# Expert 0's first three columns listed from the early rows, the rest of its list finished under its first layer, and gathers spread behind units and products

## The chip, the cores and the metric

One core of a Trainium2 chip runs the whole kernel. Its engines are TensorE (PE), VectorE (DVE), ScalarE (ACT), GpSimd (POOL) and SyncE (SP); each takes its instructions in its own order, and semaphores tie the orders together. The metric is the device time of one execution in microseconds (us), the median of three runs.

## The reference

```python
def _attn_ref(q, k, v, tau):                      # B, N, C = 4, 5056, 256
    qn = q / (norm(q, axis=1) + 1e-06);  kn = k / (norm(k, axis=1) + 1e-06)
    s = kn.transpose(0, 2, 1) @ qn / tau          # 256 x 256 for each batch
    a = exp(s - s.max(-1));  a /= a.sum(-1) + 1e-09
    return v @ a                                  # x: 4 * 5056 = 20224 rows of 256

def _moe_ref(x, w_gate, w1, w2):                  # E = 8 experts, F = 1024
    cap = N // E                                  # 2528 tokens for each expert
    order = argsort(-(x @ w_gate).flatten())
    # in this order a (token, expert) pair is taken if the token is free
    # and the expert has fewer than cap tokens
    for e in range(E):
        out[assigned == e] = maximum(x[assigned == e] @ w1[e], 0) @ w2[e]
```

Every token so goes to exactly one expert, and each expert gets exactly 2528 tokens.

## The kernel before, in words

**Attention.** The four batches' scores are made first, then the rows x = v @ a in 20 chunks of 1024 rows (`CH`), eight row tiles each (`px` products, L295; ACT copies them to `xs`, L298). ACT issues a store of every four tiles to `x_d` in DRAM (L308). The last eight chunks run in the order of `TODO`, and while they run, the routing of expert 0 is made beside them.

**Routing.** For expert p the cut of the capacity is searched on DVE, with counts summed over the partitions by small PE products (`pc`, L860 and L873). Then `compact(p)` turns the mask of 128 x 160 tokens into a list: 20 columns of 128 row numbers (`src`) and output positions (`idx`). For each column a PE product (`pi`) and a test on 160 elements with an accumulator give the position; ACT does 9 columns of the first list (L1091) and DVE 11 (L1107); some 20 small DVE operations then make `src` (L1175 to L1203) and `idx`. The list of expert p+1 is made under the products of expert p.

**Experts.** A chunk is up to four columns of 128 tokens. POOL gathers a column's rows from `x_d` with an indirect DMA (L1498, after a tiny `spacer` memset, L1497); `turn` transposes them (L1646 on PE for some chunks, DVE for others) and splits them in a high and a low part, `xH` and `xL` (L1656, L1659). `layer1` has eight units, each of six products into a `ph` buffer (L1693); ACT writes the relu's high part `hH` (L1696) and DVE the rest `hL` (L1702). `layer2` has 24 products for each column (L1742), an ACT copy to `y` (L1751), and an indirect DMA of POOL that scatters the rows to the output (L1754). For experts 4 to 7 some chunks take a variant with fewer products (`layers`, `PARTED`, `MIXED`). Expert p+1's two weight matrices come by indirect DMA on POOL too (L1390, 1 MB each), and ACT and DVE split them in a high and a low part (L1399, L1403).

**What sets the order.** A planner, `Order`, keeps an estimated clock for PE and DVE (`o.pe`, `o.dve`). Side streams (routing, lists) yield the engine and cost of their next piece, and are woven between the products where the planner thinks that the piece's inputs are ready by `o.margin` ns. `o.until(key)` runs a stream to its end at this place. Gathers wait in a list, `queue`; each call of `gather(after)` issues the next one, behind the given instruction. Before, they were called behind units of `layer1`, after scatters of `layer2`, and, in `turn` for experts with 1 in `MIXED`, all that were queued at once.

**The seam** is the place where attention ends and expert 0 begins. Before, `o.until(("idx", 0))` ended the whole first list there; then the first two columns were gathered, 26 `warm` products on an identity (L1672) ran on PE, and `turn(0, 0)` transposed the two columns with four more warm products between them. All gathers read the whole of `x_d`, so the first one waits for the last store.

Of the kernel before, what the change touches and what calls it, by code (L numbers as in the profile page):

```python
# [21 lines left out]
E, F = 8, 1024  # L22
# [11 lines left out]
FEW = 3  # L34
BY_V = 9
NACT = 9
# [7 lines left out]
PAIRS = (((0, 4), (1, 0)), ((1, 1), (1, 2)), ((1, 3), (1, 4)), ((2, 0), (2, 1)), ((2, 2), (2, 3)),  # L44
         ((2, 4), (3, 0)), ((3, 1), (3, 2)), ((3, 3), (3, 4)))
# [21 lines left out]
TODO = ((1, 1), (1, 3), (1, 4), (3, 1), (3, 2), (3, 3), (3, 4), (3, 0), (2, 0), (2, 1), (2, 2), (2, 3), (2, 4))  # L67
CUT = (4, 4, 4, 4, 4)
FIRST_CUT = (2, 4, 4, 4, 4, 2)
# [6 lines left out]
FIRST_MARGIN = 150  # L76
# [10 lines left out]
START_TICKS = 26  # L87
FILL = (4, 1)
# [22 lines left out]
def attention_moe(ctx: ExitStack, tc: tile.TileContext, q, k, vt, tau, wg, w1t, w2t, tabs, out):  # L111
# [193 lines left out]
    def store_x(b, c, xs, t0, t1):  # L305
        r0 = (b * NCH + c) * CH
        rows = x_d[r0:r0 + CH].rearrange("(p t) c -> p t c", t=T)
        nc.scalar.dma_start(rows[:, t0:t1], xs[:, t0 % TH:t0 % TH + t1 - t0, 0:C])  # L308

    with ExitStack() as sctx:  # L310
# [265 lines left out]
        late(logits, 4, behind_ac)  # L576
# [3 lines left out]
        for n in (6, 7, 5):  # L580
            late(logits, n)
# [33 lines left out]
    def route(p, R):  # L615
# [10 lines left out]
        else:  # L626
# [34 lines left out]
            for q in range(Q):  # L661
                yield (vi if q else ve)(COLS, 4)
                V.tensor_scalar(oh[:, q], f, float(E - q), None, op0=OP.is_equal)
            if few:
                need = rtile("need", (128, E))
                yield ve(R)
                V.tensor_scalar(need[:, 0:R], ne[:, 0, 0:R], row0, None, op0=OP.mult)
                yield ve(R)
                V.tensor_copy(need[:, 4:3 + R], need[:, 0:R - 1])
                yield ve(1)  # L670
                V.tensor_scalar(need[:, 3 + R:4 + R], need[:, R - 1:R], 2.0, float(COLS), op0=OP.mult, op1=OP.add)
                cnt = rtile("cnt", (128, 16))
                yield ve(R)
                V.memset(cnt[:, 3 * R:4 * R] if R > 2 else cnt, 0.0)
            else:
# [18 lines left out]
            def masked(keys, r0, r1):  # L694
                n = r1 - r0
                M = oh[:, 3:3 + n].bitcast(I16)
                if "only" not in r:
                    r["only"] = True
                    yield ve(n * COLS, 4)
                    V.tensor_scalar(M, oh[:, r0:r1], 2.0 * HALF - 1.0, -HALF, op0=OP.mult, op1=OP.add)  # L700
                mine = oh[:, 5:5 + n].bitcast(I16)
                yield ve(n * COLS, 2)
                V.tensor_tensor(mine, keys[:, None, :].to_broadcast([128, n, COLS]), M, op=OP.min)
                r["keys"] = mine
# [12 lines left out]
            def summed(slots, at):  # L717
                Ec = rtile("Ec", (128, 16), F32R)
                n = slots * R
                yield ve(n)  # L720
                V.tensor_tensor(Ec[:, 0:n].rearrange("p (j r) -> p j r", r=R), cnt[:, 0:n].rearrange("p (j r) -> p j r", r=R),
                                need[:, None, at:at + R].to_broadcast([128, slots, R]), op=OP.add)
# [3 lines left out]
                r["tot"] = pc[:, 0:n].rearrange("p (j r) -> p j r", r=R)  # L726

            def counts(tests, slots):
# [6 lines left out]
                yield from summed(slots, 0)  # L735

            def search_few(keys):
                cur = None
                own = rtile("Gf")
                yield vi(64 + COLS)  # L740
                V.scalar_tensor_tensor(own, keys, HALF, oh[:, R - 1], op0=OP.add, op1=OP.mult)
                yield from masked(keys, 0, R - 1)
                for i in range(8):
                    if i == 0:
                        thr = rtile("thr", (128, NT, CG), I16, bufs=2)[:, 0:3]
                        yield vi(3 * CG)
                        V.tensor_copy(thr, steps2[:, 0, 0:3, None].to_broadcast([128, 3, CG]))
                    bias = rtile("bias", (128, 8), bufs=2)[:, 0:3]
                    yield ve(3)
                    V.tensor_scalar(bias, thr[:, :, 0], -1.0, 0.5 - HALF, op0=OP.mult, op1=OP.add)  # L750
                    by_act = aside(own, bias, [cnt[:, j * R + R - 1:j * R + R] for j in range(3)])
                    yield from tested_by(thr, 3, cnt[:, 0:3 * R].rearrange("p (j r) -> p j r", r=R)[:, :, 0:R - 1])
                    while not by_act:
                        yield "W", 0
                    yield from summed(4, 4)
                    mx = rtile("mxc", (128, 3))
                    yield ve(3 * R, psum=True)
                    V.tensor_reduce(mx, r["tot"][:, 0:3, :], axis=AX.X, op=OP.max)
                    hit = rtile("hitc", (128, 3))
                    n = rtile("n_hit", (128, 1))  # L760
                    yield ve(64 + 3)
                    V.tensor_scalar(hit, mx, 0.0, 0.0, op0=OP.is_ge, op1=OP.add, accum_out=n)
                    step = float(1 << 14 - 2 * i)
                    new = rtile("cur", (128, 1), bufs=2)
                    yield ve(1)
                    if i == 0:
# [4 lines left out]
                    if i < 7:  # L771
                        thr = rtile("thr", (128, NT, CG), I16, bufs=2)[:, 0:3]
                        yield ve(3 * CG)
                        V.tensor_scalar(thr, steps2[:, i + 1, 0:3, None].to_broadcast([128, 3, CG]), cur, None, op0=OP.add)
# [32 lines left out]
            def search_one(keys):  # L807
# [5 lines left out]
                yield from masked(keys, 2, 3)  # L813
# [195 lines left out]
        r["G"] = ramps[p]  # L1009
        yield ve(COLS, 0.5)  # L1010
# [581 lines left out]
    def turn(p, c):  # L1592
        while any(e[:2] == (p, c) for e in queue):
            gather()
# [38 lines left out]
        if not by_v:  # L1633
# [5 lines left out]
            if not head:  # L1639
                steps.sort()  # L1640
# [417 lines left out]
```

## Time and profile before

| | |
|---|---|
| median of 3 runs | 1255.12 us (1254.25 to 1255.97) |
| the profiled execution's own time | 1257.65 us |
| its span (first to last instruction of the trace) | 1255.9 us |
| mean granted TensorE clock | 0.996 |
| PE busy | 1231.2 us, 98% |
| DVE busy | 933.7 us, 74% |
| ACT busy | 646.9 us, 52% |
| POOL busy | 382.9 us, 30% |

The profiled execution is 2.5 us above the median, and 1.75 us of its own time lie outside its span. Busy time of PE holds idle time within it, because matmuls are pipelined and their ends are modelled: a chain of 256-column products shows durations of some 0.28 us but starts one every 0.115 us. Where PE waits, the row of a timeline has the idle time before it in brackets, with what ended it.

### The profile page before, as it was taken

What the parts mean: (1) busy time and instruction counts of PE and PEld (TensorE: products, weight loads), DVE (VectorE), ACT (ScalarE), POOL (GpSimd) and SP (SyncE); (2) the same over time, 40 slices, a digit from 0 to 9 for tenths busy, and PEclk for the clock granted to TensorE, in tenths of its full rate; (3) what the DMA queues carried; (4) which work ended last, traced back from release to release, by engine and by line L of the source; (5) the groups of instructions that cost most, each with busy time, mean ns of one, the idle gap of its engine ahead of it and who ended that gap; (6) DMA issues with size and microseconds to landing.
All of it is one profiled execution on the core that took longest, in us unless ns stands there. A gap on an engine that the chain in (4) does not pass through costs nothing.

```text
span 1255.9 us, 23692 instructions
## 1 busy us (share of the span) xinstructions
PE 1231.2 (98%) x8710; PEld 1100.2 (88%) x8710; DVE 933.7 (74%) x2396; ACT 646.9 (52%) x1491; POOL 382.9 (30%) x693
## 2 busy tenths in 40 slices
PE   9999999999999999999999999999999999998998
PEld 7879977898888988988899899989989888988898
DVE  6688597798778777867867888887787777674752
ACT  5646653467324443524533755547663646563652
POOL 0000000001532363254443434433434443343422
PEclk9999999999999999999999999999999999998999
DMA  8999875436233144353533543463554362554420
GB/s 309 305 408 415 320 261 195 156 156 252 60 76 109 53 111 134 81 127 100 155 97 81 138 105 88 114 143 100 118 134 111 109 159 76 117 114 109 100 52 33
DMA packets 223812, 184.62 MB, mean 147 GB/s; under 512 B 152656, under 2 KB 193488, under 8 KB 219088
## 3 DMA queue, kind: packets, MB, share of 16 engines
q1 hardware_dynamic: 196624, 103.66, 29.7%
q0 software_dynamic: 17664, 58.22, 14.6%
q10 hardware_dynamic: 9408, 21.24, 4.4%
q8 instruction: 68, 1.11, 0.4%
q14 instruction: 48, 0.39, 0.1%
HBM read 123.30 MB, written 59.77 MB: 146 GB/s over the span
## 4 chain that ended last, share of the span: by engine, by line
PE 74%; issue 11%; POOL 6%; DMA 5%; DVE 2%; ACT 2%; POOLq 0%; SPq 0%; ACTq 0%; DVEq 0%
PE py L1742 26%; PE ph L1693 24%; PE px L295 8%; PE s L347 8%; POOL out_dram L1754 3%; DMA x_d<-xs 2%; POOL xg L1498 2%; PE pc L860 2%; PE ph L1783 2%; DMA ua<-in_q_dram 1%; PE py L1783 1%; PE px L473 1%; DMA uc<-in_k_dram 1%; PE pi L1073 1%; DMA uc<-in_q_dram 1%
## 5 line engine op out<-in xcount | busy, mean ns | idle before, releaser
L1742 PE MATMUL py<-uc,hH 128*128 128x256 f32 (+1 forms) x2560 | 341.1, 281 | 5.5 <-ACT y L1751 3.0
L1742 PEld LDWEIGHTS py<-uc,hH 128*128 128x128 f32 (+1 forms) x2560 | 316.5, 188 | 8.3 <-ACT y L1751 3.2
L1693 PE MATMUL ph<-xH,ua 128*128 128x512 f32 (+3 forms) x928 | 250.3, 387 | 0.5 <-DVE hL L1702 0.4
L1696 ACT ACTIVATE hH<-ph 128x512 fp32r<-128x512 f32 (+3 forms) x232 | 134.0, 580 | 145.9 <-PE ph L1693 134.7
L1754 POOL DMA_INDIRECT out_dram<-y,idx x105 | 109.0, 1038 | 296.9 <-ACT y L1751 270.9
L1498 POOL DMA_INDIRECT xg<-x_d,src x156 | 153.7, 985 | 138.1 <-ACT hH L1696 57.7
L1693 PEld LDWEIGHTS ph<-xH,ua 128*128 128x128 f32 x928 | 166.8, 188 | 30.4 <-DVE hL L1702 0.6
L1702 DVE SCALAR_TENSOR_TENSOR hL<-ph,hH 128x512 fp32r<-128x512 f32 (+3 forms) x232 | 153.7, 664 | 43.1 <-ACT hH L1696 36.1
L1742 PE MATMUL py<-uc,hL 128*128 128x256 f32 (+1 forms) x1280 | 181.8, 281 | 0.0
L1742 PEld LDWEIGHTS py<-uc,hL 128*128 128x128 f32 (+1 forms) x1280 | 162.4, 188 | 0.1
L1693 PE MATMUL ph<-xL,ua 128*128 128x512 f32 (+3 forms) x464 | 141.9, 385 | 0.0
L1751 ACT ACTIVATE y<-py 128x256 f32<-128x256 f32 (+1 forms) x105 | 40.2, 383 | 152.6 <-PE py L1742 120.2
L1693 PEld LDWEIGHTS ph<-xL,ua 128*128 128x128 f32 x464 | 85.3, 188 | 16.0
L347 PE MATMUL s<-ua 128*128 128x256 f32 x320 | 74.4, 389 | 3.6 <-DMA ua<-in_q_dram 2.4
L347 PEld LDWEIGHTS s<-ua 128*128 128x128 f32 x320 | 61.3, 195 | 15.9 <-issue 7.8
L298 ACT ACTIVATE xs<-px 128x512 f32<-128x512 f32 (+2 forms) x98 | 49.6, 519 | 47.7 <-PE px L295 45.7
L347 PE MATMUL s<-uc 128*128 128x256 f32 x320 | 71.5, 380 | 0.8 <-DMA uc<-in_q_dram 0.8
L347 PEld LDWEIGHTS s<-uc 128*128 128x128 f32 x320 | 60.2, 190 | 10.2 <-issue 1.8
L295 PE MATMUL px<-aH,vh 128*128 128x256 f32 (+1 forms) x232 | 67.7, 294 | 0.5 <-ACT aH L263 0.5
L295 PE MATMUL px<-aH,vl 128*128 128x256 f32 (+1 forms) x232 | 65.8, 284 | 1.7 <-DVE vl L274 1.7
L295 PE MATMUL px<-aL,vh 128*128 128x256 f32 (+1 forms) x232 | 65.8, 284 | 0.0
L1754 POOL DMA_INDIRECT out_dram<-c,idx x33 | 34.5, 1045 | 84.0 <-ACT c L1751 82.1
(431 smaller groups left out, 2137.2 us busy)
## 6 DMA issues: line engine op xcount, KB each, us to landing
x_d<-xs ACTq DMA_DIRECT2D x39, 512.0 KB
xr<-xg SPq DMA_DIRECT2D x34, 512.0 KB
xq<-xr SPq DMA_DIRECT2D x136, 128.0 KB
vr<-in_vt_dram SPq DMA_DIRECT2D x14, 1024.0 KB
uc<-in_k_dram SPq DMA_DIRECT2D x18, 512.0 KB
uc<-in_q_dram SPq DMA_DIRECT2D x18, 512.0 KB
ua<-in_k_dram SPq DMA_DIRECT2D x17, 512.0 KB
ua<-in_q_dram SPq DMA_DIRECT2D x17, 512.0 KB
```

What stands on the lines that cost most here:

```text
L295: mm = PE.matmul(px[:, i * C:i * C + width], lhsT=l_, rhs=a_, start=(j == 0), stop=(j == len(terms) - 1))
L298: S.activation(xs[:, t % TH:t % TH + n, 0:width], px[:, 0:n * width].rearrange("p (t c) -> p t c", t=n), AF.Copy)
L347: newest[0] = PE.matmul(sb[:, ib * C:(ib + 1) * C], lhsT=kt[:, t, ib * 128:(ib + 1) * 128], rhs=qt[:, t, :], start=(first and t == 0 and i ...
L860: PE.matmul(D, lhsT=ge[:, g], rhs=oh[:, 0:Q, cs_], start=(g == 0), stop=(g == COLS // CG - 1))
L1498: got = P.indirect_dma_start(out=xg[:n, i, :], out_offset=None, in_=x_d, in_offset=bass.IndirectOffsetOnAxis(ap=at, axis=0))
L1693: PE.matmul(ph[:, 0:nt], lhsT=l[:, w], rhs=x_[:, kb, 0:nt], start=(i == 0), stop=(i == 5))
L1696: relu = S.activation(hH[:, fb, 0:nt], ph[:, 0:nt], AF.Relu)
L1702: V.scalar_tensor_tensor(hL[:, fb, 0:nt], ph[:, 0:nt], 0.0, hH[:, fb, 0:nt].bitcast(F32), op0=OP.max, op1=OP.subtract)
L1742: mm = PE.matmul(py[:n, 0:C], lhsT=l[:, fb, tk], rhs=w[:, d], start=(j == 0), stop=(j == 23))
L1751: S.activation(y[:n], py[:n, 0:C], AF.Copy)
L1754: sd = P.indirect_dma_start(out=out, out_offset=bass.IndirectOffsetOnAxis(ap=idx[:n, col:col + 1], axis=0), in_=y[:n], in_offset=None)
L1783: PE.matmul(dst, lhsT=w[b][l][:, f], rhs=x[a][i], start=(first and n == 0), stop=(n == 2), skip_group_check=True)
```

## The change

1. The rows of `x_d` get an order of their own (`SLOT`), in which chunks (2, 2) and (2, 3), now the last two to be made, are the last 2048 rows. Rows 0 to 18431 (`EARLY_ROWS`) hold the other chunks.
2. A new `head_list` takes expert 0's first 384 tokens (`HEAD` = 3 columns) from the first 144 of 160 mask columns alone. The first three gathers read `x_d[0:EARLY_ROWS]`. The other 17 columns are a second list; at the seam the kernel only waits until its tests are issued (`o.until("tests")`), and its `src` and `idx` come under `layer1` of the first chunk. Their gathers, paced by a tiny ACT copy, stand behind its units.
3. The first chunk has three columns instead of two, the 26 warm products go, four stand behind the transposes; two of the last weight pieces (`OPEN`) move into units 1 and 3.
4. Gathers are called behind every second unit of `layer1` (every unit of chunk (0, 1)) and on the 17th product of a column of `layer2` (on the fifth also where the next chunks are near); those after a scatter, and the burst in `turn`, are gone.
5. The planner's margin is 0 ns for expert 0 (150 before) and 350 ns for expert 1 (700 before). The search of expert 5 is rewritten for two of its three remaining experts. Some small edits move tests between ACT and DVE.

```diff
+SLOT = {(0, c): c for c in range(NCH - 1)}
+SLOT.update({bc: NCH - 1 + 2 * s + i for s, pair in enumerate(PAIRS) for i, bc in enumerate(pair)})
+EARLY_COLS = COLS - 2 * T
+EARLY_ROWS = SLOT[2, 2] * CH
+HEAD = 3
-FIRST_CUT = (2, 4, 4, 4, 4, 2)
+FIRST_CUT = (HEAD, 4, 4, 4, 3, 2)
-FIRST_MARGIN = 150
+FIRST_MARGIN = 0
-START_TICKS = 26
-FILL = (4, 1)
+FILL = 4
+OPEN = 2
...
-        o.add(compact(p), ...)
+        o.add(compact(p) if p else head_list(), ...)
...
+    def head_list():
+        r = routed[0]
+        sc = r["sc"]
+        n = EARLY_COLS
...
+        po = pcnt.tile([128, 512], F32, name="pc")
+        yield "P", 200
+        PE.matmul(po[:, 0:1], lhsT=before, rhs=cb, start=True, stop=True)
+        PE.matmul(po[:, 128:128 + n], lhsT=follow, rhs=rem[:, 0:n], start=True, stop=True)
...
+        o.add(compact(0), lambda: COMPACT_PRIO - 1)
+        W = n + 2
+        pi = ps_c.tile([128, 512], F32, name="pi")
+        yield "P", HEAD * 75
+        for i in range(HEAD):
+            PE.matmul(pi[:, i * W:(i + 1) * W], lhsT=G[:, i * 128:(i + 1) * 128], rhs=head["E"], start=True, stop=True)
+        num = cx.tile([128, HEAD], F32, name="num_h")
+        for i in range(HEAD):
+            yield "V", 370
+            junk = rtile("junkv", dt=BF, bufs=2)
+            V.tensor_scalar(junk[:, 0:n], pi[:, i * W:i * W + n], rhalf[:, i:i + 1], 0.0, op0=OP.is_lt,
+                            op1=OP.add, accum_out=num[:, i:i + 1])
...
+        yield from rows_of(at, ext, src[:, 0:HEAD])
+        yield from tokens_of(src[:, 0:HEAD], idx[:, 0:HEAD])
+        done["head"] = True
...
-            got = P.indirect_dma_start(out=xg[:n, i, :], out_offset=None, in_=x_d,
+            got = P.indirect_dma_start(out=xg[:n, i, :], out_offset=None, in_=x_d[0:EARLY_ROWS] if (p, c) == (0, 0) else x_d,
...
     def turn(p, c):
+        o.until(("idx", 0)) if (p, c) == (0, 1) else None
+        settle()
         while any(e[:2] == (p, c) for e in queue):
             gather()
...
             want(("idx", p_), lambda: load_x(p_, c_))
-            while 1 in MIXED.get(p, ()) and queue:
-                gather()
...
-            if fb % every == 0 if p == 0 else fb > 0:
+            if (p, c) == (0, 1) or fb % 2 == (0 if (p, c) == (0, 0) or c == 0 and 1 in MIXED.get(p, ()) else 1):
                 gather(relu)
...
-                        if j in (5, 17) and p and c >= len(cuts[p]) - 2:
+                        if j in (5, 17) and not any(c + 1 in (f, f + 1) for f in MIXED.get(p, ())):
                             left = cuts[p][c] - i + (0 if c == len(cuts[p]) - 1 else cuts[p][-1])
-                            if sum(e[:2] <= (p + 1, 1) for e in queue) > (left if j == 5 else 0):
+                            urgent = (p + 1, 2 if 1 in MIXED.get(p + 1, ()) else 1)
+                            if j == 17 and queue or c >= len(cuts[p]) - 2 and sum(e[:2] <= urgent for e in queue) > left:
                                 gather(mm)
...
-            if not any(c + 1 in (f, f + 1) for f in MIXED.get(p, ())):
-                for _ in range(0 if p else 2 if queue and queue[0][1] == 0 else 1):
-                    gather()
...
-        o.until(("idx", 0))
+        o.until("tests")
...
-        load_x(0, 1, paced=True)
-        for i, q_, eng in cut_w[0][1:]:
-            split_piece(0, i, q_, eng)
-        for _ in range(START_TICKS):
-            warm()
-            o.tick(216 + 80)
+        want(("idx", 0), lambda: load_x(0, 1, paced=True))
+        while len(cut_w[0]) > 1 + OPEN:
+            split_piece(0, *cut_w[0].pop(1))
         turn(0, 0)
```

On PE at the seam, the kernel before has (`px` are attention's last products, `ph<-identr` the warm ones, `ph<-identr,xg` the transposes of the gathered columns, `ph<-xH,ua` the first layer):

```order
1199 L295 MATMUL px<-a,vr 128x256 x4
1200 L1672 MATMUL ph<-identr 128x512 x26
1201 L1646 MATMUL ph<-identr,xg 128x128 x2
1202 L1672 MATMUL ph<-identr 128x512 x4
1203 L1646 MATMUL ph<-identr,xg 128x128 x2
1204 L1672 MATMUL ph<-identr 128x512
1205 L1693 MATMUL ph<-xH,ua 128x256 x4
```

and the changed one, at the same place:

```order
1200 L301 MATMUL px<-a,vr 128x256 x4
1201 L1801 MATMUL ph<-identr,xg 128x128 x6
1202 L1827 MATMUL ph<-identr 128x512 x4
1203 L1848 MATMUL ph<-xH,ua 128x384 x4
1204 L1848 MATMUL ph<-xL,ua 128x384 x2
```

The transposes of three columns now stand right behind attention's last product; 27 of the 31 warm products are gone.

On DVE around the same place, the kernel before has (`vl` is what attention's last products wait for; `src` of 128x20 is the whole first list; the two `eq` are steps of expert 1's routing):

```order
450 L274 TENSOR_TENSOR vl<-vr,vh 128x512
...
454 L1203 COPY_PREDICATED src<-early,w__3211 128x20
455 L603 TENSOR_TENSOR eq<-L_67 128x640
...
469 L650 TENSOR_TENSOR eq<-L_67,tri 128x1120
...
478 L1659 TENSOR_TENSOR xL<-ph,xH 128x256 x2
479 L1702 SCALAR_TENSOR_TENSOR hL<-ph,hH 128x256
```

and the changed one (128x3 is the head list, 128x17 the second list):

```order
454 L1196 COPY_PREDICATED src<-early,w__3124 128x3
...
477 L280 TENSOR_TENSOR vl<-vr,vh 128x512
478 L1300 TENSOR_SCALAR at<-sgn 128x8
...
490 L1816 TENSOR_TENSOR xL<-ph,xH 128x384 x2
...
503 L1196 COPY_PREDICATED src<-early,w__3353 128x17
...
506 L656 TENSOR_TENSOR eq<-L_67,tri 128x1120
507 L1857 SCALAR_TENSOR_TENSOR hL<-ph,hH 128x384
```

The head's `src` moved ahead of attention's last two `vl`; the second list's `src` and the long `eq` moved behind `xL`, between it and the first `hL`.

On POOL, where expert 6 ends (`y` and `c` are scattered, `ub0` is the load of the second weight matrix of expert 7, `xg` are gathers; the spacer memsets ahead of each are left out), the kernel before has:

```order
539 L1390 DMA ub0_13314<-in_w2t_dram,ei_12592 128x2048
...
541 L1754 DMA out_0_dram<-y_13364,idx_11868 20224x256
...
543 L1498 DMA xg_13372<-x_d_66,src_12959 128x256
...
545 L1498 DMA xg_13372<-x_d_66,src_12959 128x256
...
547 L1498 DMA xg_13372<-x_d_66,src_12959 128x256
...
549 L1498 DMA xg_13372<-x_d_66,src_12959 128x256
...
551 L1754 DMA out_0_dram<-y_13429,idx_11868 20224x256
```

and the changed one:

```order
540 L1551 DMA ub0_13476<-in_w2t_dram,ei_12813 128x2048
...
542 L1910 DMA out_0_dram<-y_13523,idx_11626 20224x256
...
544 L1659 DMA xg_13531<-x_d_66,src_13129 128x256
...
546 L1659 DMA xg_13531<-x_d_66,src_13129 128x256
...
548 L1910 DMA out_0_dram<-y_13579,idx_11626 20224x256
...
550 L1659 DMA xg_13531<-x_d_66,src_13129 128x256
...
552 L1910 DMA out_0_dram<-y_13632,idx_11626 20224x256
...
554 L1659 DMA xg_13531<-x_d_66,src_13129 128x256
```

Four gathers in a row (543 to 549) have become two, then one after each scatter, and each now waits for a product of PE. Over the whole program POOL issues 61 gathers behind a PE product where there were 3.

## Rows read from the trace of the kernel before

**Rows 1.** The page's first part: busy time of each engine.
```profile
PE 1231.2 (98%) x8710; PEld 1100.2 (88%) x8710; DVE 933.7 (74%) x2396; ACT 646.9 (52%) x1491; POOL 382.9 (30%) x693
```

**Rows 2.** Timeline of PE at the seam: start, duration, line, count [idle before <-releaser].
```profile
309.35 1.89 PE L295 MATMUL px<-a,vr 128*128 128x256 f32 x8
311.77 6.17 PE L1672 MATMUL ph<-identr 128*128 128x512 f32 x26 [0.54 <-ACT xs L298]
318.04 0.34 PE L1646 MATMUL ph<-identr,xg 128*128 128x128 f32 x2
...
319.45 0.37 PE L1646 MATMUL ph<-identr,xg 128*128 128x128 f32 x2
...
320.21 0.90 PE L1693 MATMUL ph<-xH,ua 128*128 128x256 f32 x4
```

**Rows 3.** Timeline of POOL at the seam.
```profile
314.47 1.64 POOL L1498 DMA_INDIRECT xg<-x_d,src  x1 [23.54 <-DMA x_d<-xs]
...
316.41 1.22 POOL L1498 DMA_INDIRECT xg<-x_d,src  x1 [0.21 <-issue]
```

**Rows 4.** Timeline of ACT at the seam: two of its stores of x.
```profile
297.97 0.33 ACTq L308 DMA_DIRECT2D x_d<-xs  x1
...
311.75 0.33 ACTq L308 DMA_DIRECT2D x_d<-xs  x1
```

**Rows 5.** Timeline of DVE at the seam.
```profile
305.23 0.17 DVE L1121 TENSOR_SCALAR at<-sgn 128x9 int32<-128x9 f32 x1 [2.06 <-ACT junk L1091]
...
308.30 0.19 DVE L1203 COPY_PREDICATED src<-early,w__3211 128x20 int32<-128x20 int32 x1
...
313.96 1.32 DVE L650 TENSOR_TENSOR eq<-L,tri 128x1120 bf16<-128x1120 f32 x1
```

**Rows 6.** Windows from the seam on: stretch, length, busy time of each engine, PEclk, DMA.
```profile
311.77:320.21 8.44, 8.18 (x36) 6.01 (x36) 7.82 (x29) 0.44 (x2) 3.04 (x4) 1.00 0.20 65
320.21:334.00 13.79, 13.79 (x146) 13.58 (x146) 9.40 (x27) 5.13 (x16) 6.30 (x12) 1.00 0.19 54
```

**Rows 7.** Timeline of POOL at the end of expert 6.
```profile
1131.92 0.99 POOL L1390 DMA_INDIRECT ub<-in_w2t_dram,ei  x1 [0.30 <-issue]
...
1134.50 0.98 POOL L1498 DMA_INDIRECT xg<-x_d,src  x1 [0.22 <-issue]
...
1138.31 0.95 POOL L1498 DMA_INDIRECT xg<-x_d,src  x1 [0.22 <-issue]
...
1141.64 1.00 POOL L1754 DMA_INDIRECT out_dram<-y,idx  x1 [2.30 <-ACT y L1751]
```

**Rows 8.** Timelines of ACT at the ends of experts 5 and 6: the late copies.
```profile
1030.16 0.38 ACT L1751 ACTIVATE y<-py 128x256 f32<-128x256 f32 x1 [4.56 <-remote]
...
1140.98 0.38 ACT L1751 ACTIVATE y<-py 128x256 f32<-128x256 f32 x1 [7.40 <-issue]
```

**Rows 9.** Timeline of PE at the end of expert 6.
```profile
1135.78 1.11 PE L1742 MATMUL py<-uc,hL 128*128 128x256 f32 x8
...
1141.42 2.02 PE L1742 MATMUL py<-uc,hH 128*96 128x256 f32 x8 [3.02 <-ACT y L1751]
1143.24 1.91 PE L1742 MATMUL py<-uc,hL 128*96 128x256 f32 x8
```

**Rows 10.** Windows of the ends of experts 5 and 6, columns as in rows 6.
```profile
1020.00:1040.00 20.00, 17.80 (x121) 15.96 (x120) 11.01 (x22) 9.20 (x33) 10.27 (x18) 0.91 0.61 170
1130.00:1150.00 20.00, 16.57 (x106) 15.69 (x105) 5.99 (x10) 4.39 (x10) 11.01 (x21) 0.83 0.63 170
```

**Rows 11.** POOL and ACT at the end of expert 4: its weight load, and the next copy.
```profile
909.12 0.99 POOL L1390 DMA_INDIRECT ub<-in_w2t_dram,ei  x1 [0.30 <-issue]
...
912.52 0.39 ACT L1751 ACTIVATE y<-py 128x256 f32<-128x256 f32 x1 [0.93 <-PE py L1742]
```

**Rows 12.** PE's waits from 320 to 1250 us: total, times, longest.
```profile
PE py L1742 <- ACT y L1751: 3.0, 1, 3.0
PE pc L873 <- DVE Ex L869: 2.6, 5, 1.2
```

**Rows 13.** Durations of one DVE line: min/median/max, first and last start.
```profile
L1403 DVE TENSOR_TENSOR uc<-ub,uc x32: 676/681/693, 311.0 to 1156.3; 128x512 fp32r<-128x512 f32 x32
```

More of the change, by code (lines that the diff above doesn't have):

```diff
@@ L739, in search_few @@
+            def search_few(keys):
+                if "rows" not in r:
+                    yield from all_but_one()
+                rows, goal = r["rows"], r["goal"]
+                K = R - 1
+                n_v = 3 - BY_A[K]
                 own = rtile("Gf")
                 yield vi(64 + COLS)
-                V.scalar_tensor_tensor(own, keys, HALF, oh[:, R - 1], op0=OP.add, op1=OP.mult)
-                yield from masked(keys, 0, R - 1)
+                V.scalar_tensor_tensor(own, keys, HALF, rows[-1], op0=OP.add, op1=OP.mult)
+                thr, cur = steps2[:, 0, 0:3], None
@@ new lines, in tokens_of @@
+    def tokens_of(src, idx):
+        n = src.shape[1]
+        bt = rtile("bt", (128, NCOL))[:, 0:n]
+        yield ve(n)
+        V.tensor_scalar(bt, src, float(SLOT[1, 0] * CH), None, op0=OP.is_ge)
+        yield ve(n)
+        V.scalar_tensor_tensor(bt, src, float(SLOT[2, 0] * CH), bt, op0=OP.is_ge, op1=OP.add)
+        gap = NCH * CH - N
+        shift = 2.0
+        for b_, c_ in ((2, 4), (3, 0), (2, 2)):
+            at_ = SLOT[b_, c_] * CH
+            now = float((at_ - b_ * N - c_ * CH) // gap)
+            assert now * gap == at_ - b_ * N - c_ * CH
+            far = rtile("w2_", (128, NCOL))[:, 0:n]
+            yield ve(n)
+            V.tensor_scalar(far, src, float(at_), now - shift, op0=OP.is_ge, op1=OP.mult)
+            yield ve(n)
+            V.tensor_tensor(bt, bt, far, op=OP.add)
+            shift = now
+        yield ve(n)
+        V.scalar_tensor_tensor(idx, bt, -float(gap), src, op0=OP.mult, op1=OP.add)
@@ L1045, in compact @@
         sc = r["sc"]
+        from_ = 0 if p else HEAD
+        ncol = NCOL - from_
         cnt = sc[:, COLS - 1:COLS]
@@ L1208, in compact @@
             next_ramp(p + 1)
-        bt = rtile("bt", (128, NCOL))
-        yield ve(NCOL)
-        V.tensor_scalar(bt, src, float(NCH * CH), None, op0=OP.is_ge)
-        for b_ in range(2, B):
-            yield ve(NCOL)
-            V.scalar_tensor_tensor(bt, src, float(b_ * NCH * CH), bt, op0=OP.is_ge, op1=OP.add)
-        idx = rtile("idx", (128, NCOL), I32, bufs=3)
-        yield ve(NCOL)
-        V.scalar_tensor_tensor(idx, bt, float(N - NCH * CH), src, op0=OP.mult, op1=OP.add)
+        yield from tokens_of(src[:, from_:NCOL], idx[:, from_:NCOL])
         r["idx"] = idx
@@ L1352, in job @@
                 nphase[0] += 1
-            o.add(job(), lambda p=p: 0 if (p == 0 or done.get(("idx", p - 1))) and (
-                not done.get(("ei", p)) or done.get(("idx", p))) else EARLY_PRIO)
+            o.add(job(), lambda p=p: COMPACT_PRIO if p < 2 and done.get("head") and not done.get(("idx", 0)) else 0 if (
+                p == 0 or done.get(("idx", p - 1))) and (not done.get(("ei", p)) or done.get(("idx", p))) else EARLY_PRIO)
     scat = []
@@ L1727, in layer2 @@
         wH, wL = wt[p, 1]
-        o.until(("out", p))
+        o.until("head" if (p, c) == (0, 0) else ("out", p))
         idx = routed[p]["idx"]
@@ L1910, in attention_moe @@
             if p == 1:
+                o.margin = MARGIN // 2
+            if p == 2:
                 o.margin = MARGIN
```

323 lines of the change are left out of this document (214 added, 109 removed).

## The prediction

> **What bounds the kernel now.** I read the page's first part, and then PE's timeline, because PE is busy 1231.2 of 1255.9 us [rows 1]: a change can only gain where PE idles, runs at its low clock, or does work that isn't needed. The reader is to see three such places. The first is the seam: attention's last products start at 309.35, and the first product of expert 0 at 320.21 [rows 2]. In between PE does warm products, which compute nothing. What ends last there is the gather: POOL sat 23.54 us until the stores of x had landed, and issued its first gather at 314.47, 2.7 us behind the last store's issue at 311.75 [rows 3, 4]; the rows are transposed from 318.04 on. DVE is not late there: the whole first list stood at 308.30 [rows 5]. The second and third places are the ends of experts 5 and 6. I went to the windows whose PE clock is under 1.00, and from there to the timelines of POOL, ACT and PE: POOL issues the weight load and then gathers back to back (1134.50 to 1138.31, four of them), and the copy of y on ACT starts only at 1140.98 after 7.40 us of idling that no semaphore explains ("issue"); PE waits 3.02 us for it, and then eight products take 1.91 us where they took 1.11 [rows 7 to 9]. At 1030.16 the same copy is 4.56 us late [rows 8]. Everywhere else PE's listed waits are small: one of 3.0 us on this copy, 2.6 us on counts of the routing [rows 12].
>
> **The seam.** Removed: 27 of 31 warm products, and the dependence of the first gathers on the last stores. The head list reads only rows of earlier chunks; the last store that its gathers need is the one which stands where the store of 297.97 stands now [rows 4]. As that store's successor at 311.75 released POOL 2.7 us later [rows 3, 4], the first gather can go at about 300.7, if DVE has the head's `src` by then. I put that `src` at 299 to 303 (36 added DVE operations ahead of it and among attention's `vl`, of 0.17 us each as the short ones [rows 5], some 6 us in all, of which DVE's idle 2.06 us covers a third). Three gathers at 1.64 us are issued by 305.6 to 308, and the last lands about 1.9 us behind the end of its issue (314.47 + 1.64 to 318.04 [rows 2, 3]), 307.5 to 310. Attention's products end at 311.2 (309.35 + 1.89), and the head list's six small products add about 0.4 us. So the rows are there, and the transposes follow the 0.54 us wait on ACT that the warm products have now: 6 of them, estimated at 0.09 us each (half of a 256-column product's 0.115 and a little more), end at 312.7. From the last transposes to the first product of layer 1 it is 0.76 us now (319.45 to 320.21), which makes 313.4 in place of 320.21: **6.8 us earlier**. The four warm products stand in that 0.76 us and cost nothing; the third column is work moved forward.
>
> What is late next is DVE. The second list's `src` (15 short operations, 1.5 to 2.5 us) and the long `eq` (1.32 us [rows 5]) now stand between `xL` and the first `hL`; behind it two split pieces of 0.68 us [rows 13] and more of `eq` stand among the eight `hL`. PE's eight units take 48 products of some 0.17 us (an estimate between 256 and 512 columns), 8.2 us, and layer 2 wants the last `hL` 1.8 us later, at +10; I add up DVE's queue to +11 to +12.5. ACT's in-order `pace` copies wait for the second `src` as well, and hold the relus behind them by 1 to 2 us. DVE's slack now is 2.06 us before [rows 5], 0.62 in the seam and 4.39 in the 13.79 us behind it [rows 6], 7.1 together against the 6 added. So most of it is hidden, and I take 2 us of PE waiting, between 0 and 5: **-4.8 us, from -6.8 to -1.8**. If DVE's cover were gone, all 6 us would fall on PE.
>
> **The gathers.** The burst leaves the ends of experts 5 and 6. In its place gathers alternate with scatters, each behind a product of PE. What the freezes cost is read in two windows of 20 us [rows 10]: PE idles 2.20 and 3.43 us, and the granted clock of 0.91 and 0.83 means time at the lower of its two levels (1.2 and 2.4 GHz) that loses 0.09 and 0.17 of 20 us, 1.8 and 3.4 us. Together 10.8 us. Why should they go? The end of expert 4 has the same weight load at 909.12 and no burst, and its next copy of y waits 0.93 us for nothing but its products [rows 11]. ACT resumes at 1140.98 [rows 8], about where the last gather of the burst lands (1138.31 + 0.95 + 1.9). So load and scatter alone don't freeze ACT, load and burst do. I leave 1.3 us of the 10.8 for what the load still does: **-9.5 us, from -10.8 to 0**. A gather that waits for the 17th product holds the scatter behind it on POOL; that product is over 7 products, 0.8 us, before the copy of y which the scatter waits for, and a gather takes 0.95 us, so a scatter comes about 0.2 us later, under POOL's idle time. The rows that these gathers fetch are wanted a chunk later.
>
> **Margins and the rest.** With a margin of 0 and 350 ns the planner puts counts of the routing nearer to their inputs. The trace has five waits of 2.6 us in all on them [rows 12], 0.52 us each. Three more would be 1.6 us; none, or five of the longest (1.2 us), are the ends. I take **+1.5, from 0 to +6**. The rewritten search of expert 5, the nine `tokens_of` operations where there were four and the tests moved to DVE run under PE's products; a loss there would show as a wait on DVE, and it is within these ends.
>
> **The sum.** -4.8 - 9.5 + 1.5 = -12.8 us on the profiled execution's 1257.65 (span 1255.9 and 1.75 around it), 1244.85. That execution is 2.5 us above the median of 1255.12, so in terms of medians **1242.3 us**.
>
> **One rule against it.** The split of weights, a subtraction of two SBUF operands, took 676 to 693 ns in all of its 32 runs, those beside indirect DMAs among them [rows 13]. The Trainium skill, SBUF — State Buffer, section "Who interferes with whom", says that a VectorE instruction with two SBUF inputs contends with a GpSimd instruction that reads SBUF, and that the second to issue waits for the whole of the first. By that rule the 58 gathers moved on to products could each hold DVE for their 0.95 us, 55 us of DVE time, and it would make the next rival likelier. No row here stretches by anything like it, so I give it no weight of its own.
>
> **The rivals.** *Seam only* (17%): the freeze belongs to the load, or to indirect DMAs in that place whatever their order, and stays. For it: four indirect DMAs still follow within the same column, and "issue" names no cause. Against: the end of expert 4. It gives -4.8 + 1.5 = -3.3, 1251.8 us.
>
> *Freezes only* (10%): DVE's queue at the seam eats the gain. For it: DVE is busy 7.82 of 8.44 us there [rows 6], and POOL and ACT wait for it too. Against: 4.39 us of idling right behind. It gives -9.5 + 1.5 - 0, 1247.1 us.
>
> *Slower* (11%): what stops ACT is the mixture itself, gathers close to scatters while copies of y run, and the change carries it from 3 gathers behind products to 61, behind more of the weight loads. Then the two freezes stay and others come; at the price of the smaller of the two (2.20 + 1.8 = 4.0 us), two new ones give -4.8 + 1.5 + 8.0 = +4.7, 1259.8 us. It decides from one new freeze on: with the old ones kept, 3.3 us more eat the seam's gain. For it: both copies that are late now are copies of y among scatters [rows 8]. Against: in layer 2 a scatter and a gather for each column ran before also, and PE's list has a single wait on a copy of y [rows 12].
>
> *As forecast* (62%): 1242.3 us, by itself 1237.5 (-6.8 - 10.8 + 0 on 1255.12) to 1248.5 (seam -2, freezes -7.5, margins +3).
>
> **How the numbers follow.** The range starts at the low end of the forecast and reaches over both one-sided cases to 1254.5; out of it are the slower case and a few hundredths at either end. A difference under 0.2%, 2.5 us, can't be told from none. Faster by more than that (below 1252.6): the forecast, freezes only, and 10 of the 17 hundredths of seam only, 0.82. Slower (above 1257.6): 0.10 of the 0.11. Between: 0.08.
>
> **What would show it.** Right: a first gather near 301 that waits for an earlier store or for DVE's `src`; transposes within 1.5 us of the last `px`; layer 1 at about 313.5; PEclk 1.00 at the ends of experts 5 and 6, and copies of y there within 1 us of their products. Wrong: a first gather after 306, or gaps of over 3 us in the first layer's products while `hL` is late; half clock at either end, or at a new place; PE's waits on `pc` above 5 us in all.

## The result: the change is 0.64% slower

The changed kernel took 1263.98 us (median of 6 runs, 1260.64 to 1271.76) against 1255.79 of the kernel before; the ratio is 1.0064, with a 95% interval of 1.0035 to 1.0093. The forecast was 1242.3. The profiled execution is the slowest of the six, 1271.76 us (span 1270.0), and the clock granted to PE has a part in the spread: this run has 0.992, one of 1261.68 us has 0.999, which over the span is some 9 us (an estimate). The run at 0.999 still lies 19 us above the forecast.

The page's first part, which answers to [rows 1]:

```profile
PE 1232.2 (97%) x8688; PEld 1103.6 (87%) x8688; DVE 936.6 (74%) x2603; ACT 637.8 (50%) x1445; POOL 381.8 (30%) x694
```

PE has the same work and more idle time. Of PE's waits from 320 us on, which answer to [rows 12], these are the largest (total, times, longest):

```profile
PE pc L935 <- DVE Ex L931: 5.4, 7, 2.7
PE py L1897 <- ACT p L1907: 4.7, 2, 3.4
PE ph L1848 <- DVE xL L1793: 4.4, 2, 3.3
PE pi L1252 <- DVE G L1243: 2.4, 2, 1.5
```

Two new kinds stand there: a wait of layer 1 and of layer 2 for the next chunk's rows (`xL`; `p`, which ACT could not copy since it stood behind `xH` of these rows), and more waits on counts.

**The ends of experts 5 and 6** are as forecast: PE is never idle there and has its full clock, where [rows 10] have 17.80 and 16.57 us of 20.

```profile
1040.00:1060.00 20.00, 20.00 (x136) 18.03 (x135) 14.60 (x28) 12.67 (x40) 9.73 (x18) 1.00 0.43 140
1150.00:1170.00 20.00, 20.00 (x132) 18.32 (x131) 10.83 (x19) 9.00 (x18) 10.88 (x21) 1.00 0.46 147
```

**The seam.** PE, POOL and ACT, which answer to [rows 2 to 4]:

```profile
312.76 0.81 PE L1801 MATMUL ph<-identr,xg 128*128 128x128 f32 x6
...
315.99 1.49 PE L1848 MATMUL ph<-xH,ua 128*128 128x384 f32 x4 [1.42 <-ACT xH L1813]
...
321.01 0.86 PE L1848 MATMUL ph<-xH,ua 128*128 128x384 f32 x4
```

```profile
305.09 0.95 POOL L1659 DMA_INDIRECT xg<-x_d,src  x1 [12.78 <-DMA x_d<-xs]
```

```profile
314.05 1.34 ACTq L314 DMA_DIRECT2D x_d<-xs  x1
315.45 0.87 ACT L1813 ACTIVATE xH<-ph 128x384 fp32r<-128x384 f32 x2 [1.42 <-PE ph L1827]
```

The gathers go before the last stores, and the transposes follow attention at once. But ACT spends 1.34 us on issuing the last store (0.33 before), `xH` comes behind it, PE idles 1.42 us, and its clock falls: four products take 1.49 us and not 0.86. Layer 1 starts 4.2 us earlier than before (315.99 against 320.21), not 6.8.

That belongs to this execution and not to the kernel. Runs e2 and e8 below have the same instructions in the same order up to here; in their profiles the store's issue takes 0.33 us, PE keeps its full clock, and layer 1 starts at 312.13 and 313.33 (e3 has the 1.34 us too). In the profiles of e4 to e7, which keep the seam of before, it starts at 318.68 to 319.79. The seam so gains 5 to 8 us.

DVE at the seam, which answers to [rows 5], and the windows, which answer to [rows 6]:

```profile
318.69 0.18 DVE L1196 COPY_PREDICATED src<-early,w__3353 128x17 int32<-128x17 int32 x1
...
319.01 1.32 DVE L656 TENSOR_TENSOR eq<-L,tri 128x1120 bf16<-128x1120 f32 x1
320.25 0.55 DVE L1857 SCALAR_TENSOR_TENSOR hL<-ph,hH 128x384 fp32r<-128x384 f32 x1
```

```profile
311.77:320.21 8.44, 7.02 (x31) 6.10 (x30) 8.39 (x26) 3.67 (x10) 0.83 (x1) 0.80 0.34 126
320.21:334.00 13.79, 13.79 (x120) 13.74 (x118) 11.03 (x42) 4.81 (x13) 8.36 (x16) 1.00 0.23 67
```

DVE is idle for 0.05 and 2.76 us there, where it had 0.62 and 4.39.

The whole list stands 10.4 us later than before (318.69 against 308.30), and the long `eq`, the entry to expert 1's search, 5.0 us later (319.01 against 313.96), although PE is 4.2 us ahead. The first count of that search, as PE's timeline has it in the kernel before and in the changed one:

```profile
326.08 0.23 PE L873 MATMUL pc<-Ex,ones_q 128*128 128x128 f32 x1
```

```profile
334.72 0.33 PE L935 MATMUL pc<-Ex,ones_q 128*128 128x128 f32 x1 [0.53 <-DVE Ex L931]
```

8.6 us later (in the profiles of e1, e2 and e8 it comes at 330.88 to 332.29, still 5 to 6 us later). The search stays behind: the cut of expert 1 is known at 400.3 (395.1 before), that of expert 2 at 510.4 (490.5). The list of expert 1 is no later than before (`src` at 429.4, 432.3 before); those of experts 2, 3 and 4 are, at 543.7, 663.2 and 766.6 (531.3, 639.1 and 729.8). What a late list does shows at 582 us, in SP's, DVE's and PE's timelines of the changed kernel:

```profile
577.17 2.92 SPq L1649 DMA_DIRECT2D xq<-xr  x4
```

```profile
583.30 1.32 DVE L1782 STREAM_TRANSPOSE ph<-xq 128x512 f32<-128x512 f32 x2 [2.56 <-DMA xq<-xr]
```

```profile
585.43 1.36 PE L1848 MATMUL ph<-xH,ua 128*128 128x512 f32 x4 [3.32 <-DVE xL L1793]
...
587.44 1.91 PE L1848 MATMUL ph<-xH,ua 128*128 128x512 f32 x4
```

The rows of the second chunk land after DVE has come to their transpose; DVE holds everything behind it, PE idles 3.32 us, and its clock falls (four products take 1.91 us, 1.07 at 591). The eight gathers of expert 2's first two chunks stand behind products and between scatters here: the last is issued at 572.57, 28.9 us behind the list. The other new place is the end of expert 0, where the gathers and scatters of POOL bunch, seven in a row from 432.10 to 440.85, and DVE, then PE, stop as ACT did at the ends of experts 5 and 6:

```profile
443.98 0.21 DVE L925 TENSOR_TENSOR Dm<-pc,dmask 128x48 f32<-128x48 f32 x1 [5.07 <-remote]
```

```profile
444.77 0.45 PE L935 MATMUL pc<-Ex,ones_q 128*128 128x96 f32 x1 [2.75 <-DVE Ex L931]
...
447.71 1.91 PE L1897 MATMUL py<-uc,hL 128*96 128x256 f32 x8
```

### The profile page after: what moved, and what is told of

It is laid out like the page before. It is cut to its first block, busy times and chain, and to the rows that moved or that the text cites. A ratio compares the mean times of both kernels' runs of the same rounds, so it can differ in the third digit from the quotient of the medians.

```text
span 1270.0 us, 23822 instructions
## 1 busy us (share of the span) xinstructions
PE 1232.2 (97%) x8688; PEld 1103.6 (87%) x8688; DVE 936.6 (74%) x2603; ACT 637.8 (50%) x1445; POOL 381.8 (30%) x694
## 4 chain that ended last, share of the span: by engine, by line
PE 79%; DMA 6%; issue 5%; DVE 4%; ACT 2%; POOL 2%; another core or an unknown queue 1%; SPq 1%; ACTq 0%; POOLq 0%; DVEq 0%
PE py L1897 28%; PE ph L1848 23%; PE s L353 8%; PE px L301 8%; PE ph L1936 3%; PE py L1936 3%; DMA x_d<-xs 2%; PE pc L922 2%; DMA ua<-in_q_dram 1%; POOL out_dram L1910 1%; PE px L479 1%; DMA xq<-xr 1%; DMA uc<-in_k_dram 1%; PE pi L1252 1%
## 5 line engine op out<-in xcount | busy, mean ns | idle before, releaser
L1848 PEld LDWEIGHTS ph<-xH,ua 128*128 128x128 f32 x928 | 169.9, 190 | 38.4 <-DVE xL L1793 5.5
L369 DVE TENSOR_TENSOR acc_k<-acc_k,sq 128x1024 f32<-128x1024 f32 x36 | 43.9, 1219 | 18.3 <-ACT sq L368 17.8
```

The costliest lines, as they stand in the source:

```text
L369: V.tensor_tensor(acc, acc, sq, op=OP.add)
L1848: PE.matmul(ph[:, 0:nt], lhsT=l[:, w], rhs=x_[:, kb, 0:nt], start=(i == 0), stop=(i == 5))
```

## The experiments

All were timed in 5 rounds beside the kernel before on the same chip. That kernel took 1251.88 us on the chip of the first four, 1255.10 on that of the next four, 1255.53 on that of the next three, and 1251.56 on that of the last, so ratios are compared, and a difference between runs of different chips is taken from their ratios.

| run | what | us | ratio to before (95%) |
|---|---|---|---|
| | the change | 1263.98 | 1.0064 (1.0035 to 1.0093) |
| e1 | the change, margins of before | 1281.99 | 1.0248 (1.0223 to 1.0273) |
| e2 | the change, placement of before without burst | 1266.81 | 1.0123 (1.0102 to 1.0144) |
| e3 | both | 1296.41 | 1.0349 (1.0330 to 1.0369) |
| e4 | before without burst | 1262.47 | 1.0080 (1.0065 to 1.0094) |
| e5 | before with the change's placement | 1250.95 | 0.9960 (0.9941 to 0.9979) |
| e6 | before with expert 1's routing delayed | 1286.76 | 1.0250 (1.0226 to 1.0275) |
| e7 | before with the change's margins | 1265.20 | 1.0074 (1.0050 to 1.0098) |
| e8 | the change, still smaller margins | 1265.12 | 1.0070 (1.0048 to 1.0093) |
| e9 | the change, 26 warm products put back | 1252.24 | 0.9977 (0.9967 to 0.9986) |
| e10 | the change, 5 subtractions on POOL | 1246.62 | 0.9934 (0.9921 to 0.9947) |
| e11 | e5, 8 subtractions on POOL | 1254.00 | 0.9990 (0.9979 to 1.0001) |
| e12 | the change, 3 subtractions on POOL | 1246.71 | 0.9964 (0.9951 to 0.9978) |

**e1 to e4: the first theories.** I first took the new waits at their word: small margins make the waits on counts, and spread gathers make the rows late.

```diff
-FIRST_MARGIN = 0
+FIRST_MARGIN = 150
-                o.margin = MARGIN // 2
+                o.margin = MARGIN
```

> The changed kernel with the planner's margins of before (150 ns for expert 0, 700 from expert 1 on). Margin theory: PE's waits on counts of the routing between 330 and 570 us (7 us in the profile of the changed kernel, and 3.4 us of half clock behind the longest) go: 1253 to 1257 us. Gather theory (rows that are gathered later land late, and the transposes of DVE hold everything behind them): those waits are not what matters, 1261 to 1265. List theory (the head list and the tests and searches that moved load DVE too much): 1261 to 1265 as well.

Measured: 1281.99, by the ratios 23 us more than the change and not 10 less. The margin theory fell, and the wrong way round: smaller margins had bought time. Of the gather theory the number fell, but not the mechanism: PE's longest waits in this run are for rows (`xH` 5.2 us, `xL` 4.4 us).

e2 puts the calls of `gather` back behind units `fb > 0` and scatters, as in the kernel before:

```diff
-            if (p, c) == (0, 1) or fb % 2 == (...):
+            if (p, c) == (0, 1) or (fb % 2 == 0 if (p, c) == (0, 0) else fb % every == 0 if p == 0 else fb > 0):
...
+            if not any(c + 1 in (f, f + 1) for f in MIXED.get(p, ())):
+                for _ in range(0 if p else 2 if queue and queue[0][1] == 0 else 1):
+                    gather()
```

> The changed kernel with its gathers placed as before: behind units of layer 1 (from the second on) and after scatters, but without the burst of before in the turn of experts 5 to 7. Gather theory: the waits for rows at 582, 709, 885 and 1067 us go (10 us, with 3.4 us of half clock), 1250 to 1255 us. Margin theory: 1261 to 1265, with the waits on counts of 334 to 570 us still there.

Measured: 1.0123 where the change has 1.0064. That doesn't clear the spreading, because the edit has no burst either, and e4 below shows what that costs by itself. PE's largest wait in e2 is of e4's kind, 7.15 us at 1057.58 and 5.13 at 1170.13 (7.01 and 5.74 in e4):

```profile
PE py L1897 <- ACT p L1906: 12.3, 2, 7.1
```

The wait at 582 is gone, as the gather theory had it: the same eight gathers are all issued by 557.65, 18.5 us behind their list. The table behind e12 shows where e2 wins and loses.

> Both edits: margins and gathers of before, no burst; what is left of the change are the head list, the seam, the third column of the first chunk and the rewritten search. If margins and gathers are all of the loss: 1243 to 1247, as the prediction had it. List theory: 1252 or more, with waits on DVE left.

e3 has the edits of e1 and e2. Measured: 1296.41, so with the margins of before the rest of the change (head list, seam, third column, searches) costs more time still. PE's waits show a late search of expert 5, for which the planner can do no more than wait:

```profile
PE pc L901 <- issue: 5.4, 1, 5.4
PE pc L901 <- DVE Ec L898: 4.3, 3, 2.7
```

e4 is the kernel before without the burst:

```diff
-            while 1 in MIXED.get(p, ()) and queue:
-                gather()
```

> The kernel before without the burst of gathers in the turn of experts 5 to 7; those gathers go to the next units. If the burst is what froze ACT at the ends of experts 5 and 6: 1244 to 1248 us, with the clock at 1.00 there. If the freeze belongs to the weight load or to anything else in that place: 1253 to 1258.

Measured: 1262.47. The freeze is gone where the burst was (the window 1020 to 1040 has PE busy throughout at clock 1.00), so the burst did freeze ACT; but it was there for a reason. Its rows are now gathered a stage later, and DVE waits for them, and PE behind DVE, longer than the freeze was:

```profile
1050.63 1.30 DVE L1546 STREAM_TRANSPOSE xg<-xq 128x512 f32<-128x512 f32 x2 [7.96 <-DMA xq<-xr]
```

```profile
1052.92 2.08 PE L1740 MATMUL py<-uc,hH 128*128 128x256 f32 x8 [7.01 <-ACT p L1749]
```

**e5 to e8: the second theory.** The routing is a chain of DVE and PE beside the experts, and the change makes it late from expert 1 on; late lists make late rows. Rival: gathers and margins by themselves.

e5 is the kernel before with no burst, no gathers after scatters, and the change's two rules for units and products.

> The kernel before with the change's placement of gathers alone (behind every second unit, on the 17th and where urgent the 5th product of a column; no burst, none after scatters). Lateness theory (the change makes the lists of tokens late, and late lists make gathers and rows late; the placement itself is good): no freeze at the ends of experts 5 and 6, 1242 to 1248 us. Rival, that spreading the gathers makes rows late by itself: 1256 or more, with PE's waits of 3 us or more in layer 2 of experts 6 and 7.

Measured: 0.9960, 5.0 us (2.6 to 7.4) faster. The placement is good, if less than forecast: at the ends of experts 5 and 6 PE is busy 19.82 and 20.00 of 20 us, but a new wait of PE, 2.44 us before 452.27, stands at the end of expert 0, with half clock behind it (0.50 from 454 to 456), although the routing is on time there (cut of expert 1 at 394.4, 395.1 before).

```diff
-            yield ve(COLS, ptr=1)
-            V.scalar_tensor_tensor(w, khi, base, klo, op0=OP.subtract, op1=OP.add)
+            for _ in range(25 if p == 1 else 1):
+                yield ve(COLS, ptr=1)
+                V.scalar_tensor_tensor(w, khi, base, klo, op0=OP.subtract, op1=OP.add)
```

> The kernel before with one step of expert 1's routing (160 elements on DVE, some 0.3 us) done 25 times in place of once, which adds about 8 us of DVE work and delay to that routing and changes nothing else. Lateness theory: expert 1's list and all lists behind it come 8 us or more later, 1257 to 1270 us. If the routing has room to absorb it: 1250 to 1254.

Measured: 31 us slower. In its trace expert 1's cut comes 13.5 us later (408.5 for 395.1), expert 2's 23.3 us later (513.8 for 490.5), and PE waits for the second chunk of expert 2 as in the change, only longer:

```profile
PE ph L1694 <- DVE xL L1631: 9.1, 2, 6.3
```

A delay of one routing is thus not paid once. It is not paid at each list either: by the table behind e12, 14 us are lost at the end of expert 0, 11 up to the first copy of expert 2, and 11 up to the end of expert 5.

> The kernel before with the change's margins alone (0 for expert 0, 350 ns for expert 1). Lateness theory: lists come earlier, but nothing waits for them in this kernel, 1249 to 1254 us. If small margins cost PE waits on counts, as the prediction had it: 1253 to 1258.

e7 is the reverse of e1's edit, on the kernel before. Measured: 1265.20, 9.3 us slower, against what the lateness theory expected and more than the prediction had: its largest wait on a count (4.09 us before 445.38; the longest before is 1.2) stands beside eight indirect DMAs in a row (434.30 to 443.88), and DVE, on which the count waits, stopped for 5.01 us with no semaphore that explains it. So the larger part of this loss is a stop like those at the ends of experts, and not the margin's own waits.

```diff
-            if p == 1:
-                o.margin = MARGIN // 2
             if p == 2:
-                o.margin = MARGIN
+                o.margin = MARGIN // 2
```

> The changed kernel with still smaller margins: 0 for experts 0 and 1, 350 ns from expert 2 on (700 in the change). Lateness theory: lists come earlier again, 1252 to 1260 us. If margins are too small already: 1264 or more.

Measured: 1265.12, ratio 1.0070, as the change. The lists come nearly as early as before (expert 3's at 643.3, expert 4's at 732.1), but there are waits on counts in their place: 2.74 us before 441.90, where DVE has stopped for 5.1 us as in e7, and 1.87 before 561.75. So margins choose where a late routing is paid, and lateness of lists alone isn't the whole cause.

**e9 to e12: giving DVE its time back.**

```diff
+        for _ in range(26):
+            warm()
+            o.tick(216 + 80)
         turn(0, 0)
```

> The changed kernel with 26 warm products put back between attention's last product and the transposes: about 6 us of work that computes nothing, in which DVE gets on with the routing of expert 1. Lateness theory (the change gains at the seam by taking from DVE the time that the routing needs): what is lost at the seam comes back at the later waits, 1256 to 1264 us. If the loss behind the seam has nothing to do with that time: 1269 to 1271 (1264 and the added work).

Measured: 1252.24, by the ratios 11 us less than the change. Six us of products that compute nothing make it faster. The first count of expert 1 is back at 325.91, and the later waits go with it:

```profile
325.91 0.22 PE L935 MATMUL pc<-Ex,ones_q 128*128 128x128 f32 x1
```

```profile
PE pc L935 <- DVE Ex L931: 3.2, 6, 1.4
PE pi L1252 <- ACT ext L1327: 2.0, 3, 0.8
PE ph L1848 <- DVE xL L1816: 1.4, 1, 1.4
```

e10 leaves the seam as the change has it and takes work off DVE instead:

```diff
+        elif p == 0 and (i, q_) in ((0, 0), (0, 1), (0, 2), (1, 2), (1, 3)):
+            low(P)
```

> The changed kernel with 5 of the 8 subtractions of expert 0's weight split on POOL in place of DVE, which takes 3.3 us off DVE around the seam. Lateness theory: the first count of expert 1's search comes 3 us or more earlier (335 us in the profile of the change), and the whole is 3 to 12 us faster, 1252 to 1261 us. If DVE's load at the seam doesn't matter: 1262 to 1266.

Measured: 1246.62, ratio 0.9934 (0.9921 to 0.9947): 16 us under the change, and the fastest of all kernels against its reference. Layer 1 starts at 314.03, the first count comes at 328.50, and no half clock follows from 327 us to the end of the experts.

```profile
328.50 0.22 PE L935 MATMUL pc<-Ex,ones_q 128*128 128x128 f32 x1
```

> The kernel before with the change's placement of gathers and all 8 of those subtractions on POOL, as a candidate that beats both kernels. Lateness theory: DVE gains 5 us around the seam, lists come earlier, 1245 to 1250 us. If only the placement counts: 1250 to 1252.

e11 (the edit `low(P)` for all 8, on e5). Measured: 0.9990, worse than e5. In its trace PE waits 3.82 us for `vl` up to 310.26, beside POOL's subtractions, and layer 1 starts at 324.93 (319.79 in e5): what went off DVE's list came back as waiting at the seam. Taking work off DVE is no good by itself; which work, and beside what, decides.

> The changed kernel with only the first three subtractions on POOL; the two that ran there under the first layer are on DVE again. In the profile of the run with five, DVE operations of 0.1 to 0.2 us that ran beside these two took 1.95 us and ended with them, and PE waited 1.25 and 0.94 us for hL right behind. If POOL's subtractions hold DVE's operations: these waits go, 1243 to 1246 us. If those two ran on POOL for nothing but gain: 1247 to 1250.

e12 has the first three of e10's five pieces. Measured: 1246.71, but on a chip where the kernel before takes 1251.56, so 0.9964. The waits for `hL` are gone, as the first theory had it, but the time lies between the two ranges, and against its reference it is no gain over e10. What the two pieces are worth stays open.

**Where each run loses.** ACT's copies of layer 2's output (`y`, `c`, `p` from `py`) are the same 184 in the same order in all of these runs, so the start of one of them says how far a run is. The table has five, with their start in the kernel before, and how many us later (+) or earlier (-) each run makes them. Each row is one profiled execution, so 2 or 3 us are no finding.

| run | copy 18, expert 0 (444.55) | copy 21, expert 1 (478.79) | copy 41, expert 2 (599.28) | copy 125, end of expert 5 (1022.03) | copy 161, expert 7 (1170.62) |
|---|---|---|---|---|---|
| the change | -4.4 | +1.5 | +8.6 | +18.9 | +14.1 |
| e2 | -7.5 | -2.8 | -0.2 | +2.4 | +9.2 |
| e4 | -2.5 | -1.1 | -1.4 | -2.3 | +5.2 |
| e5 | -0.9 | +4.8 | +3.8 | +3.5 | -6.5 |
| e6 | -5.4 | +8.4 | +19.6 | +30.8 | +27.9 |
| e9 | +4.2 | +5.6 | +4.1 | +4.3 | -5.6 |
| e10 | -2.2 | +0.5 | -1.4 | -1.5 | -11.3 |

From copy 18 to copy 125 the change loses 23 us, e2 10, and e9 and e10 less than 1. So at the change's lateness most of the loss takes two things together, a routing that is late and gathers that wait for products: e9 and e10 take the first away, e2 the second (its list of expert 2 is 4.5 us earlier as well). With a longer delay the placement of before loses too: e6, 36 us. From copy 125 to copy 161, past the two ends where the kernel before freezes, the spread placement gains 10 us in e5, e9 and e10 (5 in the change itself), and the placement of before without the burst loses 7 in e2 and e4.

## Why the prediction was wrong

**The step that failed** is "DVE's slack now is 2.06 us before, 0.62 in the seam and 4.39 behind it, 7.1 together against the 6 added. So most of it is hidden". It asked only whether DVE would be in time for `hL`. In the warm 8.4 us DVE was busy 7.82, and but for 1.7 us of a weight split what it did there was the routing of expert 1, in the kernel before:

```profile
315.31 0.96 DVE L653 TENSOR_SCALAR eq<-eq 128x160 bf16<-128x160 bf16 x7
316.31 0.85 DVE L603 TENSOR_TENSOR eq<-eq 128x640 bf16<-128x640 bf16 x2
...
317.83 0.97 DVE L663 TENSOR_SCALAR eq<-f 128x160 bf16<-128x160 bf16 x8
...
319.05 0.78 DVE L891 TENSOR_TENSOR ge<-hi,th 128x1200 bf16<-128x1200 int16 x1
```

Bringing PE forward, and moving the second list behind `xL`, both take from that: the first count came at 334.72, not 326.08, and the search of expert 2 began behind time (first count at 424.48, 416.50 before) and lost more at the end of expert 0. "If DVE's cover were gone, all 6 us would fall on PE" was wrong in kind. e6 priced a delay of that routing at 31 us; e9 and e10 gave the time back, by idling PE or by relieving DVE, and got 11 and 16 us for it. That DVE's time at the seam decides is shown by these two.

**The second step that failed** is "The rows that these gathers fetch are wanted a chunk later", which put the spreading at nothing outside the two ends. With a list that is late by some 12 us the rows landed after DVE had come to them (2.56 us at 583.30, PE idle for 3.32); with gathers placed as before the wait is not there (e2). How much of the 23 us is the late routing by itself, and how much the spreading, isn't separated: no run has the change's routing on time and the placement of before with its burst.

**The seam itself** was right, in its mechanism and, up to layer 1, in its size: the store's issue of 1.34 us is luck of this execution, and e2 and e8 start layer 1 at 312.13 and 313.33, where 313.4 was forecast. What was wrong in it is when the first gather goes: 2.7 us behind the store was taken from the last store, and it is 6.8 us (298.28 to 305.09; 6.6 to 6.9 in e1, e2, e3, e8 and e9). It did no harm, since the three gathers were still in time.

**The freezes** went from the ends of experts 5 and 6, as forecast, and burst and freeze belong together (e4, e5). The size of -9.5 us holds for the two ends (10 us in e5, e9 and e10 by the table). What the sum lacked is the new stop at the end of expert 0, which takes 5.7 us of it in e5, so that placement alone is worth 5.0 us. It came in e5 with a routing that was on time, so the stop in the change is not shown to be the routing's doing.

**The margins**, put at +1.5 us from 0 to +6, were the second miss. On the kernel before they cost 9.3 us (e7), most of it in the stop at 445; in the change they save 23 (e1 against the change). A margin trades waits on counts against late lists, and I priced the first alone.

**The rivals.** *Slower* was given 11%, for gathers close to scatters and new freezes behind more of the weight loads; one new stop came, at 444 us, with no weight load in its row of DMAs, but the main cause was in none of the rivals. "Freezes only" named DVE's queue at the seam, and stopped at the seam.

## What to carry to other kernels

When PE's idle stretch is cut away, ask what the other engines did in it, and when that is next needed: a stretch in which a second engine is 93% busy is no slack, even if PE does nothing there. A side chain that runs one stage ahead of the main work has to be timed as a second critical path, by its first step and by when each stage's result is ready, because a delay there returns at later stages. A burst of transfers that stalls an engine may be what brings the next stage's data in time: look at what lands last before it is spread. A total can hide this: e2 lost in the last two experts what it had won in the six before.

## What the runs showed of the hardware

In e10 the POOL subtraction at 317.97 held a DVE operation of 17 elements, which takes 0.17 us elsewhere, for 1.95 us; it ended 0.06 us after POOL's. DVE's rows and POOL's:

```profile
317.38 1.95 DVE L1213 TENSOR_SCALAR w__3379<-src 128x17 f32<-128x17 int32 x1
...
320.37 1.88 DVE L683 TENSOR_SCALAR eq<-f 128x160 bf16<-128x160 bf16 x5
```

```profile
317.97 1.30 POOL L1564 TENSOR_TENSOR uc<-ub,uc 128x512 fp32r<-128x512 f32 x1
...
320.43 1.31 POOL L1564 TENSOR_TENSOR uc<-ub,uc 128x512 fp32r<-128x512 f32 x1
```

The second subtraction holds DVE's group of five in the same way (1.88 us, where six of that shape take 0.75 at 315.83 in the same run). The first row begins 0.59 us ahead of POOL's, beside an indirect DMA that ends at 317.95, so which came first isn't settled by it. Two rows ahead of the seam in the same run do settle it; here DVE's operation begins behind POOL's:

```profile
301.05 1.28 POOL L1564 TENSOR_TENSOR ua<-ub,ua 128x512 fp32r<-128x512 f32 x1 [0.98 <-ACT ext L1273]
303.52 1.29 POOL L1564 TENSOR_TENSOR ua<-ub,ua 128x512 fp32r<-128x512 f32 x1 [1.19 <-ACT ua L1560]
```

```profile
301.20 1.15 DVE L1215 TENSOR_TENSOR bt<-bt,w__3167 128x3 f32<-128x3 f32 x1
...
303.55 1.44 DVE L1095 SCALAR_TENSOR_TENSOR klo<-asg,cs,klo 128x160 f32<-128x160 f32 x1
```

They take 0.16 and 0.38 us elsewhere, and end 0.02 and 0.18 us after POOL's. The Trainium skill, SBUF — State Buffer, section "Who interferes with whom", has this: the two engines share a pair of ports, and the second to come waits for the whole of the first's instruction. For POOL's arithmetic the trace agrees on the size of the hold and, in the last two rows, on the order; the 32 rows of the prediction beside indirect DMAs show none.

Stops that no semaphore explains ("remote", "issue") stood behind five to eight indirect DMAs issued with pauses of 0.2 to 0.6 us: at 1030 and 1141 us in the kernel before, at 444 in the change (5.07 us on DVE), at 444 in e7 (5.01 on DVE), and, with no loss on PE, at 442 in the kernel before (5.49 on ACT). They were not isolated by a run of their own, so their cause stays open. In e9 and e10 ACT's relus and PE's products part the gathers there, and the stop is not seen. Last, the same program's runs lie 11 us apart in the change (1260.64 to 1271.76) and 5.7 in the kernel before. The clock is one reason: a stop like that of 3.32 us at 585 is followed by products at half clock, so a run gets longer by more than the stop. It is not the only one, since runs of 1265.92 and 1271.76 us both have 0.992.
